# The last unit of q and k in 4 tiles of 112 tokens, the last pair of v in 8 tiles of 120, and an output with filler tokens

## The chip, the cores and the metric

The kernel runs on one core of a Trainium2 chip. A core has a matrix engine (TensorE, PE in the profile), a vector engine (VectorE, DVE), a scalar engine (ScalarE, ACT), a general engine (GpSimd, POOL) and a sync engine (SyncE, SP), which here does nothing but issue DMA transfers. Operands lie in an on-chip memory of 128 partitions, matmul results in eight PSUM banks. The metric is device time in microseconds (us) for one launch, the median of several runs.

## The reference

Four batches (B = 4) of 5056 tokens (N) with 256 channels (C) go through an attention over channels, and all 20224 resulting tokens through a soft mixture of experts with 8 experts of 4 slots.

```python
def _attn_ref(q, k, v, tau):                      # q, k, v: (4, 5056, 256)
    qn = q / (np.linalg.norm(q, axis=1, keepdims=True) + 1e-06)
    kn = k / (np.linalg.norm(k, axis=1, keepdims=True) + 1e-06)
    s = kn.transpose(0, 2, 1) @ qn / tau          # 256 x 256 a batch: a sum over all tokens
    a = softmax over the last axis of s
    return v @ a
def _moe_ref(x, phi, w1, w2):                     # x: (20224, 256), phi: (256, 32)
    logits = x @ phi
    d = softmax over the tokens (axis 0) of logits
    slots = d.T @ x                               # 32 slots, 4 for each of 8 experts
    slot_out = relu(slots @ w1[e]) @ w2[e]        # for each expert e, w1[e]: 256 x 1024
    c = softmax over the slots (axis 1) of logits
    return c @ slot_out                           # (20224, 256)
```

## The kernel before, in words

**Units.** The scores of a batch are a sum over its tokens, so q and k are read in units of 512 tokens (10 to a batch, 40 in all, `u`): a tile `raw` of 128 partitions, with 4 tiles of 128 tokens, and q and k beside each other (1 MB a unit). 5056 is 9 x 512 + 448. The tenth unit (`u % 10 == 9`, units 9, 19, 29 and 39) therefore has three tiles of 128 tokens and a half tile of 64 (`HD`), and is loaded by two DMAs: `qk3` (128 partitions, 768 KB, line 128) and `qkh` (64 partitions, 128 KB, line 129). There are five `raw` buffers, and a unit is loaded when the one five before it is done.

For each unit ACT rounds the first two tiles into `hl` (`cast`, line 202), DVE subtracts to get the remainder (`low`, line 208), PE forms the scores (`score`: lines 258 and 259 for those two tiles, line 252 for the other two, which are used unrounded), ACT squares the unit (`square`, lines 224, 226, 227) and DVE adds the squares up for the norms (`add`, lines 234, 235, 237). In a tenth unit `square` and the upper half of `add` are each split into an instruction for 128 partitions and one for 64.

**Pairs.** v is read in pairs of units, 8 tiles of 128 tokens (5 pairs to a batch, `p`), each by two DMAs of 512 KB (line 141). The fifth pair (`p % 5 == 4`) has 7 tiles of 128 and one of 64: its second half takes a DMA of 384 KB (line 143) and one of 64 KB on 64 partitions (`vh`, line 145). v is also wanted transposed: some pairs load it so (lines 151 and 153), for others PE transposes tiles (`turn`, line 406) and ACT copies them out (`turned`, line 413). `logits` (line 428) multiplies the transposed v with `M` (attention times phi) into a PSUM bank `L`. The places of L that stand for no token in a fifth pair get -1e30 by a memset (line 423). Exponentials of the logits (`weights`, `exps`) then weigh v in `gather` (line 537).

**The end.** After the last batch the slots go through the experts' weights `w1` and `w2` (16 DMAs of 1 MB). The output of a pair is formed on PE (`out_mul`, line 764), copied from PSUM by ACT (line 791) and DVE (line 793), and stored. Four pairs of a batch are stored as 128 partitions x 8 KB (lines 800 and 802, the first four pairs of batch 0 in two halves). The fifth is stored as a 768 KB piece on 128 partitions (`ob6`, line 804) and a 192 KB piece on 96 partitions (`oh`, line 805).

**What sets the order.** Every step is an entry of a `plan`, and a list `ORDER` of 1059 numbers, written out by hand, says in which order the entries are issued. Each engine works through its own instructions in that order. All loads and stores are issued by SP, in order. An instruction waits by semaphores. Eight of these (DMAHW0 to DMAHW7 in the listings below) are shared by the transfers in turn, so that a transfer also waits for the one eight before it.

Of the kernel before, what the change touches and what calls it, by code (L numbers as in the profile page):

```python
# [81 lines left out]
def colnorm_attention_soft_moe(  # L82
    ctx: ExitStack,
    tc: tile.TileContext,
    qk: bass.AP,
    qk3: bass.AP,
    qkh: bass.AP,
    v8: bass.AP,
    v7: bass.AP,
    vh: bass.AP,  # L90
    vt8: bass.AP,
    vt7: bass.AP,
    few: bass.AP,
    w1: bass.AP,
    w2: bass.AP,
    oa: bass.AP,
    ob6: bass.AP,
    oh: bass.AP,
):
# [19 lines left out]
    raws, sqs = {}, {}  # L119

    def load_qk(u, parts=((0, 4),)):
        b, i = divmod(u, UB)
        raw = apool.tile([P, 4, 2, C], F32, tag="raw", name=f"raw{u}", bufs=NRAW)
        if i < UB - 1:
            for lo, hi in parts:
                sp.dma_start(raw[:, lo:hi], qk[b, i][:, lo:hi])
        else:
            sp.dma_start(raw[:, 0:3], qk3[b])
            sp.dma_start(raw[:HD, 3], qkh[b])
        raws[u] = raw  # L130

    vs, vts = {}, {}

    def load_v(p, h):
        b, i = divmod(p, PB)
        if p not in vs:
            vs[p] = slot("v" if p < 17 else "raw", f"v{p}")
        vt = vs[p]
        lo, hi = 4 * h, 4 * h + 4
        if i < PB - 1:  # L140
            sp.dma_start(vt[:, lo:hi], v8[b, i][:, lo:hi])
        else:
            sp.dma_start(vt[:, lo : min(hi, 7)], v7[b][:, lo : min(hi, 7)])
            if h:
                sp.dma_start(vt[:HD, 7], vh[b])

    def load_vt(p, m):
        b, i = divmod(p, PB)
        t = vt_tile(p, m)
        if i < PB - 1:  # L150
            sp.dma_start(t, vt8[b, i, m])
        else:
            sp.dma_start(t[:, : 8 * P - HD], vt7[b, m])
# [44 lines left out]

    def cast(u):
        ns = NS[u]  # L200
        hl = apool.tile([P, 2, 4, C], F32R, tag="hl", name=f"hl{u}", bufs=3)
        act.copy(hl[:, :ns, 0::2, :], raws[u][:, :ns])  # L202
        hls[u] = hl

    def low(u):
        ns = NS[u]
        hl = hls[u]
        dve.tensor_tensor(  # L208
            hl[:, :ns, 1::2, :], raws[u][:, :ns], hl[:, :ns, 0::2, :].bitcast(F32), op=ALU.subtract
        )  # L210

    sqtag = {}
# [7 lines left out]

    def square(u):
        sq = apool.tile([P, 4, 2, C], F32, tag=f"sq{sqtag[u]}", name=f"sq{u}")
        if u % UB < UB - 1:
            act.activation(sq, raws[u], AF.Square)  # L224
        else:
            act.activation(sq[:, 0:3], raws[u][:, 0:3], AF.Square)
            act.activation(sq[:HD, 3], raws[u][:HD, 3], AF.Square)
        sqs[u] = sq

    def add(u, lo, hi):  # L230
        b, i = divmod(u, UB)
        a, s = sqs[b * UB], sqs[u]
        if i == UB - 1 and hi == 4:
            dve.tensor_tensor(a[:, lo:3], a[:, lo:3], s[:, lo:3], op=ALU.add)
            dve.tensor_tensor(a[:HD, 3], a[:HD, 3], s[:HD, 3], op=ALU.add)
        else:
            dve.tensor_tensor(a[:, lo:hi], a[:, lo:hi], s[:, lo:hi], op=ALU.add)  # L237

    def score(u, j):
        b, i = divmod(u, UB)  # L240
        if "S" not in st[b]:
            st[b]["S"] = [bank(S0, f"S{b}_0"), bank(S1, f"S{b}_1")]
            st[b]["open"] = [True, True]
        pc = HD if i == UB - 1 and j == 3 else P
        for m in range(2):
            sm = st[b]["S"][m]
            cols = slice(P * m, P * m + P)
            first = st[b]["open"][m]
            st[b]["open"][m] = False
            if j >= NS[u]:  # L250
                raw = raws[u]
                pe.matmul(  # L252
                    sm[:, :C], raw[:pc, j, 1, cols], raw[:pc, j, 0, :], start=first, stop=False, skip_group_check=True
                )
# [146 lines left out]
    def turn(p, h, m, tb):  # L401
        tp = bank(tb, f"vTp{p}_{h}_{m}")
        n = 0
        for jj in range(4):
            pc = HD if p % PB == PB - 1 and h == 1 and jj == 3 else P
            pe.transpose(tp[:, n : n + pc], vs[p][:pc, 4 * h + jj, P * m : P * m + P], ident[:pc, :pc])  # L406
# [11 lines left out]
    def logits(p, lb):  # L418
        b, q = divmod(p, PB)
        M = st[b]["M"]  # L420
        L = bank(lb, f"L{p}")[:, : 8 * S].rearrange("p (j s) -> p j s", s=S)
        if q == PB - 1:
            dve.memset(L[HD:, 7, :], -1e30)
        for m in range(2):
            x = vts[p, m].rearrange("p (j w) -> p j w", w=P)
            for g in range(G):
                n = 7 if q == PB - 1 and g >= 2 else 8
                pe.matmul(  # L428
                    L[S * g : S * g + S, :n, :],
                    M[:, m, :],  # L430
                    x[:, :n, S * g : S * g + S],
                    start=m == 0,
                    stop=m == 1,
                )
        Ls[p] = L
# [316 lines left out]
    ots, ops = {}, {}  # L752
# [21 lines left out]
    def out_evict(b, p, hf, g):  # L774
        if (b, p) not in ots:
            ots[b, p] = slot(OT[b * PB + p], f"o{b}_{p}")
        ot = ots[b, p]
        if p < PB - 1:
            dst = ot.rearrange("p q (w c) -> p (q w) c", w=2).rearrange("p (x gh) c -> p gh x c", x=2)
            dst = dst[:, 2 * g : 2 * g + 2]  # L780
            src = ops[b, p, hf, g]
            if hf is None:
                src = src.rearrange("p h (x c) -> p h x c", x=2)
            else:
                dst = dst[:, :, hf]
        else:
            lo, step = (2 * g, 1) if g < 2 else (g + 2, 2)
            dst = ot[:, lo : lo + step + 1 : step, :]
            src = ops[b, p, hf, g]
        if g % 2 == 0:  # L790
            act.copy(dst, src)  # L791
        else:
            dve.tensor_copy(dst, src)  # L793

    def store(b, p, hf):
        ot = ots[b, p]
        if p < PB - 1:
            o2 = ot.rearrange("p (x q) c -> p x (q c)", x=2)
            if hf is None:
                sp.dma_start(oa[b, p], o2)  # L800
            else:
                sp.dma_start(oa[b, p][:, hf], o2[:, hf])
        else:
            sp.dma_start(ob6[b], ot[:, 0:6])
            sp.dma_start(oh[b], ot[:96, 6:8])
# [49 lines left out]
    for p in range(14):  # L855
# [6 lines left out]
        b, gi, x, n = group(p)  # L862
# [185 lines left out]
    t = 41.0  # L1048
# [13 lines left out]
    for x in ORDER:  # L1062
        key, _, f, a = plan[x]
# [66 lines left out]
```

## Time and profile before

| | |
|---|---|
| median of 3 runs | 304.97 us (303.45 to 307.35) |
| the profiled execution | 304.32 us, of which the span from first to last instruction is 302.5 us |
| granted TensorE clock, mean | 0.957 |
| busy share of the span | PE 86%, DVE 77%, ACT 65%, POOL 9% |
| DMA | 110.38 MB, 365 GB/s over the span (89.29 MB read, 20.71 MB written) |

The profile gives for each engine the time it was busy, in total and in 40 slices of the span; PEclk is the clock granted to TensorE in each slice, in tenths of full speed, and the DMA row the mean busy share of the core's 16 DMA engines. Groups of instructions are listed by line, engine, operation and tile, with count, total and mean duration. A wait is put down to the instruction or transfer that came last before the waiting engine went on. A matmul's ends are modelled, so a busy PE need not be at its peak.

### The profile page before, as it was taken

How to read it: one execution, taken by the hardware profiler on the slowest of the kernel's cores; microseconds unless marked ns; L12 is line 12 of the kernel's file. 1: busy time of each engine (PE TensorE's matmuls, PEld its weight loads, DVE VectorE, ACT ScalarE, POOL GpSimd, SP SyncE). 2: the span in 40 equal slices, each digit the busy share in tenths (PEclk: the TensorE clock that was granted, in tenths of full speed). 3: DMA queues.
4: the chain of work that ended last, by engine and by line, in shares of the span. 5: the costliest groups of instructions: out<-in, count | busy, mean ns of one | idle time of the engine just before them, and what ended most of it. 6: DMA issues, size and time to landing. Idle time of an engine off the chain costs nothing. (4 is left out here: it accounts for less than half of the span.)

```text
span 302.5 us, 5958 instructions
## 1 busy us (share of the span) xinstructions
PE 260.6 (86%) x2358; PEld 199.4 (66%) x2358; DVE 233.2 (77%) x387; ACT 196.1 (65%) x290; POOL 28.1 (9%) x18
## 2 busy tenths in 40 slices
PE   4999899999999988998999999999989999984000
PEld 3788687877768874875887687777655588763000
DVE  1599959999989979986999999567887547997000
ACT  2996969798879694675886976366840526865000
POOL 0000002000002403000222000133202030000000
PEclk9999799999999999999999999999999999999555
DMA  6999999999999998799899989699999718999996
GB/s 237 427 430 415 374 405 420 371 389 366 423 398 360 417 390 319 280 356 422 281 407 405 385 310 378 248 351 422 406 347 400 305 71 341 404 422 399 420 430 261
DMA packets 21707, 110.38 MB, mean 365 GB/s; under 512 B 2608, under 2 KB 2864, under 8 KB 13616
## 3 DMA queue, kind: packets, MB, share of 16 engines
q1 hardware_dynamic: 21680, 110.01, 92.4%
q8 instruction: 18, 0.29, 0.4%
q14 instruction: 9, 0.07, 0.1%
HBM read 89.29 MB, written 20.71 MB: 364 GB/s over the span
## 5 line engine op out<-in xcount | busy, mean ns | idle before, releaser
L252 PE MATMUL S<-raw 128*128 128x256 f32 (+1 forms) x328 | 82.4, 391 | 6.4 <-DMA raw<-in_qk_dram 4.8
L237 DVE TENSOR_TENSOR sq<-sq,sq 128x1024 f32<-128x1024 f32 (+1 forms) x59 | 81.2, 1393 | 3.2 <-ACT sq L224 2.3
L224 ACT ACTIVATE sq<-raw 128x2048 f32<-128x2048 f32 x36 | 68.7, 1914 | 14.9 <-DMA raw<-in_qk_dram 9.4
L252 PEld LDWEIGHTS S<-raw 128*128 128x128 f32 (+1 forms) x328 | 60.4, 195 | 17.1 <-DMA raw<-in_qk_dram 5.9
L258 PE MATMUL S<-hl 128*128 128x512 f32 x156 | 64.7, 444 | 1.8 <-DVE hl L208 1.8
L208 DVE TENSOR_TENSOR hl<-raw,hl 128x1024 fp32r<-128x1024 f32 x39 | 49.0, 1271 | 8.4 <-ACT hl L202 8.3
L202 ACT CAST hl<-raw 128x1024 fp32r<-128x1024 f32 x39 | 40.4, 1044 | 7.1 <-DMA raw<-in_qk_dram 4.8
L259 PE MATMUL S<-hl 128*128 128x256 f32 x156 | 44.0, 282 | 0.0
L258 PEld LDWEIGHTS S<-hl 128*128 128x128 f32 x156 | 29.6, 190 | 10.5 <-DVE hl L208 2.6
L259 PEld LDWEIGHTS S<-hl 128*128 128x128 f32 x156 | 29.8, 191 | 0.6
L406 PE MATMUL vTp<-ident,v 128*128 128x128 f32 (+1 forms) x160 | 23.4, 277 | 1.7 <-DMA v<-in_v_dram 1.7
L537 PE MATMUL G<-v,dn 128*32 128x256 f32 (+1 forms) x320 | 23.3, 382 | 0.0
L406 PEld LDWEIGHTS vTp<-ident,v 128*128 128x128 f32 (+1 forms) x160 | 18.2, 141 | 6.7 <-issue 3.0
L764 PE MATMUL op_None<-so,cT 32*128 32x256 f32 x256 | 19.6, 397 | 2.3 <-ACT o L791 1.2
L305 POOL TENSOR_TENSOR rn<-rn,half 128x4 f32<-128x4 f32 x4 | 6.8, 1701 | 154.5 <-DVE rn L300 119.8
L793 DVE COPY o<-op_None 128x512 f32<-128x512 f32 x32 | 20.0, 679 | 1.3 <-issue 1.0
L791 ACT COPY o<-op_None 128x512 f32<-128x512 f32 x32 | 17.1, 591 | 5.1 <-PE op_None L764 1.9
L764 PEld LDWEIGHTS op_None<-so,cT 32*128 32x128 f32 x256 | 15.1, 184 | 6.4 <-PE op_None L764 3.2
L428 PE MATMUL L<-vt,M 128*32 128x256 f32 (+1 forms) x272 | 18.2, 381 | 1.1 <-issue 1.1
L413 ACT COPY vt<-vTp 128x512 f32<-128x512 f32 (+1 forms) x28 | 15.8, 576 | 4.0 <-PE vTp L406 2.8
L537 PEld LDWEIGHTS G<-v,dn 128*32 128x32 f32 (+1 forms) x320 | 12.4, 109 | 6.4 <-issue 1.2
L635 POOL TENSOR_TENSOR nat<-nat,cm 128x1280 f32<-128x1280 f32 x4 | 11.2, 2803 | 30.8 <-DVE cm L632 17.5
(119 smaller groups left out, 284.2 us busy)
## 6 DMA issues: line engine op xcount, KB each, us to landing
raw<-in_qk_dram SPq DMA_DIRECT2D x35, 1024.0 KB, 9.1
v<-in_v_dram SPq DMA_DIRECT2D x36, 512.0 KB, 8.3
w<-in_moe_w_dram SPq DMA_DIRECT2D x16, 1024.0 KB, 9.0
out_dram<-o SPq DMA_DIRECT2D x12, 1024.0 KB, 9.5
vt<-in_vt_dram SPq DMA_DIRECT2D x16, 512.0 KB, 9.5
out_dram<-o SPq DMA_DIRECT2D x8, 512.0 KB, 4.1
raw<-in_qk_dram SPq DMA_DIRECT2D x4, 768.0 KB, 8.0
out_dram<-o SPq DMA_DIRECT2D x4, 768.0 KB, 8.0
```

The costliest lines, as they stand in the source:

```text
L202: act.copy(hl[:, :ns, 0::2, :], raws[u][:, :ns])
L208: dve.tensor_tensor(hl[:, :ns, 1::2, :], raws[u][:, :ns], hl[:, :ns, 0::2, :].bitcast(F32), op=ALU.subtract)
L224: act.activation(sq, raws[u], AF.Square)
L237: dve.tensor_tensor(a[:, lo:hi], a[:, lo:hi], s[:, lo:hi], op=ALU.add)
L252: pe.matmul(sm[:, :C], raw[:pc, j, 1, cols], raw[:pc, j, 0, :], start=first, stop=False, skip_group_check=True)
L258: pe.matmul(sm, hl[:, j, 2, cols], rhs, start=first, stop=False, skip_group_check=True)
L259: pe.matmul(sm[:, :C], hl[:, j, 3, cols], hl[:, j, 0, :], start=False, stop=False, skip_group_check=True)
L406: pe.transpose(tp[:, n : n + pc], vs[p][:pc, 4 * h + jj, P * m : P * m + P], ident[:pc, :pc])
L428: pe.matmul(L[S * g : S * g + S, :n, :], M[:, m, :], x[:, :n, S * g : S * g + S], start=m == 0, stop=m == 1,)
L537: pe.matmul(gp[S * g : S * g + S, :C], dn[:pc, x, j, :], vt[:pc, j, :], start=x == 0 and j < G, stop=x == n - 1 and j >= G,)
L764: pe.matmul(ops[b, p, hf, g][:, h, :], cT[b][S * g : S * g + S, 4 * i : 4 * i + 4, :].rearrange("s j t -> s (j t)"), so[S * g : S * g + S] ...
L793: dve.tensor_copy(dst, src)
```

## The change

The 448 tokens of a tenth unit become 4 tiles of 112 (`PQ`), the 960 tokens of a fifth pair of v 8 tiles of 120 (`PV`). The unit is one DMA of 896 KB on 112 partitions, the pair two DMAs of 480 KB on 120 partitions. The host passes the arrays `qk7` and `v7` in that shape; `qkh` and `vh` are gone. `cast`, `low`, `square`, `add` and `score` run on 112 partitions, with one instruction where there were two. `turn` transposes 120 columns at a time, `logits` reads tiles of 120 tokens, where the fourth group of each has 24 tokens in place of 32, and the memset fills the 8 empty columns of that group in all 8 tiles. `gather` runs over 120 partitions. The output of a fifth pair is copied and stored like any other, as 8 tiles of 128 tokens of which the last 8 are filler, in one DMA of 1024 KB; the host drops the filler. `ORDER` is as it was.

```diff
@@ load_qk
-            sp.dma_start(raw[:, 0:3], qk3[b])
-            sp.dma_start(raw[:HD, 3], qkh[b])
+            sp.dma_start(raw[:PQ], qk7[b])
@@ load_v
-            sp.dma_start(vt[:, lo : min(hi, 7)], v7[b][:, lo : min(hi, 7)])
-            if h:
-                sp.dma_start(vt[:HD, 7], vh[b])
+            sp.dma_start(vt[:PV, lo:hi], v7[b][:, lo:hi])
@@ cast (low likewise)
+        n = P if u % UB < UB - 1 else PQ
-        act.copy(hl[:, :ns, 0::2, :], raws[u][:, :ns])
+        act.copy(hl[:n, :ns, 0::2, :], raws[u][:n, :ns])
@@ square
-            act.activation(sq[:, 0:3], raws[u][:, 0:3], AF.Square)
-            act.activation(sq[:HD, 3], raws[u][:HD, 3], AF.Square)
+        act.activation(sq[:n], raws[u][:n], AF.Square)
@@ add
-            dve.tensor_tensor(a[:, lo:3], a[:, lo:3], s[:, lo:3], op=ALU.add)
-            dve.tensor_tensor(a[:HD, 3], a[:HD, 3], s[:HD, 3], op=ALU.add)
+        dve.tensor_tensor(a[:n, lo:hi], a[:n, lo:hi], s[:n, lo:hi], op=ALU.add)
@@ turn
-            pc = HD if p % PB == PB - 1 and h == 1 and jj == 3 else P
+            pc = PV if p % PB == PB - 1 else P
@@ logits
-            dve.memset(L[HD:, 7, :], -1e30)
+            dve.memset(L[S * (G - 1) :, :, w - P :], -1e30)
...
-                n = 7 if q == PB - 1 and g >= 2 else 8
+                n = min(S, w - S * g)
                 pe.matmul(
-                    L[S * g : S * g + S, :n, :],
+                    L[S * g : S * g + S, :, :n],
@@ gather
-            pc = HD if q == PB - 1 and j == 7 else P
+            pc = PV if q == PB - 1 else P
@@ store
-            sp.dma_start(ob6[b], ot[:, 0:6])
-            sp.dma_start(oh[b], ot[:96, 6:8])
+            sp.dma_start(oa[b, p], o2)
```

Three places show what this does to the engines' instructions. SP, where unit 9 is loaded (`raw_232`) between unit 8 (before it) and unit 10 (`raw_270`, `raw_269` after the change), before and then after; in brackets what a transfer waits for:

```order
L156 DMA few_sb<-in_few_dram 128x67
L128 DMA raw_232<-in_qk_dram 128x1536 [waits DVE_49,DMAHW6_49,PE_49,Activation_49]
L129 DMA raw_232<-in_qkh_dram 64x512 [waits DMAHW7_49]
L126 DMA raw_270<-in_qk_dram 128x2048 [waits DVE_49,DMAHW0_49,PE_49,Activation_49]
L141 DMA v_272<-in_v_dram 128x1024 [waits DMAHW1_49]
```

```order
L150 DMA few_sb<-in_few_dram 128x67
L125 DMA raw_232<-in_qk_dram 112x2048 [waits DVE_49,DMAHW6_49,PE_49,Activation_49]
L123 DMA raw_269<-in_qk_dram 128x2048 [waits DVE_49,DMAHW7_49,PE_49,Activation_49]
L137 DMA v_271<-in_v_dram 128x1024 [waits DMAHW0_49]
```

The transfer of 64 partitions is gone, nothing else changed place, and from here on every transfer waits for a semaphore one further back in the turn of eight.

SP at the end of the program, where the last pairs are stored, before and after:

```order
L800 DMA out_dram<-o_0_2754 128x2048 [waits DMAHW7_49]
L800 DMA out_dram<-o_3_2910 128x2048 [waits DMAHW0_49,DVE_49,Activation_49]
L804 DMA out_dram<-o_4_2925 128x1536 [waits DMAHW1_49,DVE_49,Activation_49]
L805 DMA out_dram<-o_4_2925 96x512 [waits DMAHW2_49]
L1116 UNCONDITIONAL_BRANCH
```

```order
L785 DMA out_dram<-o_0_2737 128x2048 [waits DMAHW4_49]
L785 DMA out_dram<-o_3_2891 128x2048 [waits DMAHW5_49,DVE_49,Activation_49]
L785 DMA out_dram<-o_4_2906 128x2048 [waits DMAHW6_49,DVE_49,Activation_49]
L1086 UNCONDITIONAL_BRANCH
```

The last two transfers are one, of full size.

DVE, where the squares of unit 19 (`sq_702`, `sq_697` after) are added and the logits `L` of a fifth pair masked, before and after:

```order
L456 TENSOR_REDUCE mxs_1_729<-L_664 128x1
L237 TENSOR_TENSOR sq_356<-sq_356,sq_702 128x1024
L234 TENSOR_TENSOR sq_356<-sq_356,sq_702 128x512
L235 TENSOR_TENSOR sq_356<-sq_356,sq_702 64x512
L423 MEMSET L_755 64x32
L208 TENSOR_TENSOR hl_733<-raw_633,hl_733 128x4x256
```

```order
L447 TENSOR_REDUCE mxs_1_723<-L_659 128x1
L227 TENSOR_TENSOR sq_353<-sq_353,sq_697 112x1024 x2
L414 MEMSET L_748 32x8x8
L204 TENSOR_TENSOR hl_727<-raw_628,hl_727 128x4x256
```

Three additions are two, and what follows them on DVE is the same.

More of the change, by code (lines that the diff above doesn't have):

```diff
@@ L17 @@
 P, S, G = 128, 32, 4
+PQ, PV = 112, 120
 UB = 10
@@ L85, in colnorm_attention_soft_moe @@
     qk: bass.AP,
-    qk3: bass.AP,
-    qkh: bass.AP,
+    qk7: bass.AP,
     v8: bass.AP,
     v7: bass.AP,
-    vh: bass.AP,
     vt8: bass.AP,
@@ L232, in add @@
         a, s = sqs[b * UB], sqs[u]
[L233 to L237, printed above, removed]
+        n = P if i < UB - 1 else PQ
+        dve.tensor_tensor(a[:n, lo:hi], a[:n, lo:hi], s[:n, lo:hi], op=ALU.add)
     def score(u, j):
@@ L243, in score @@
             st[b]["open"] = [True, True]
-        pc = HD if i == UB - 1 and j == 3 else P
+        pc = PQ if i == UB - 1 else P
         for m in range(2):
@@ L256, in score @@
                 hl = hls[u]
-                rhs = hl[:, j, 0:2, :].rearrange("p x c -> p (x c)")
-                pe.matmul(sm, hl[:, j, 2, cols], rhs, start=first, stop=False, skip_group_check=True)
+                rhs = hl[:pc, j, 0:2, :].rearrange("p x c -> p (x c)")
+                pe.matmul(sm, hl[:pc, j, 2, cols], rhs, start=first, stop=False, skip_group_check=True)
                 pe.matmul(
-                    sm[:, :C], hl[:, j, 3, cols], hl[:, j, 0, :], start=False, stop=False, skip_group_check=True
+                    sm[:, :C], hl[:pc, j, 3, cols], hl[:pc, j, 0, :], start=False, stop=False, skip_group_check=True
                 )
@@ L796, in store @@
         ot = ots[b, p]
[L797 to L802, printed above, removed]
[L803 to L805 removed]
+        o2 = ot.rearrange("p (x q) c -> p x (q c)", x=2)
+        if hf is None:
+            sp.dma_start(oa[b, p], o2)
+        else:
+            sp.dma_start(oa[b, p][:, hf], o2[:, hf])
     def fill(b, k):
@@ L1083 @@
     x = np.stack([q, k], axis=2)
-    n9, n3 = 9 * UT, 3 * P
+    n9 = 9 * UT
     add("qk", x[:, :n9].reshape(B, 9, 4, P, 2, C).transpose(0, 1, 3, 2, 4, 5))
-    add("qk3", x[:, n9 : n9 + n3].reshape(B, 3, P, 2, C).transpose(0, 2, 1, 3, 4))
-    add("qkh", x[:, n9 + n3 :])
-    n4, n7 = 4 * 2 * UT, 7 * P
+    add("qk7", x[:, n9:].reshape(B, 4, PQ, 2, C).transpose(0, 2, 1, 3, 4))
+    n4 = 4 * 2 * UT
     add("v8", v[:, :n4].reshape(B, 4, 8, P, C).transpose(0, 1, 3, 2, 4))
-    add("v7", v[:, n4 : n4 + n7].reshape(B, 7, P, C).transpose(0, 2, 1, 3))
-    add("vh", v[:, n4 + n7 :])
+    add("v7", v[:, n4:].reshape(B, 8, PV, C).transpose(0, 2, 1, 3))
     add("vt8", v[:, :n4].reshape(B, 4, 2 * UT, 2, P).transpose(0, 1, 3, 4, 2))
@@ L1103 @@
         add(name, inputs[name])
-    flat = nc.dram_tensor("out_0_dram", (B * N * C,), F32, kind="ExternalOutput").ap()
-    cuts = np.cumsum([0, B * 4 * P * 8 * C, B * P * 6 * C, B * 96 * 2 * C])
-    shapes = [(B, 4, P, 2, 4 * C), (B, P, 6, C), (B, 96, 2, C)]
-    pats = [
[3 rows of a table removed]
-    ]
-    for x_, (lo, hi) in enumerate(zip(cuts[:-1], cuts[1:])):
-        sh = shapes[x_]
-        names = pats[x_].split("->")[1].split()
-        args.append(flat[int(lo) : int(hi)].rearrange(pats[x_], **dict(zip(names[1:], sh[1:]))))
+    out_ap = nc.dram_tensor("out_0_dram", (B, PB, P, 2, 4 * C), F32, kind="ExternalOutput").ap()
+    args.append(out_ap)
     with tile.TileContext(nc, schedule_with_timeline_sim=True) as tc:
@@ L1118 @@
     r = run_bass_kernel_spmd(nc, [arrays], core_ids=[0])
-    o = np.asarray(r.results[0]["out_0_dram"]).reshape(-1)
-    oa, ob, oh = (o[int(lo) : int(hi)].reshape(sh) for lo, hi, sh in zip(cuts[:-1], cuts[1:], shapes))
-    out = np.empty((B, N, C), np.float32)
-    out[:, :n4] = oa.reshape(B, 4, 4, S, 2, G, 2, P).transpose(0, 1, 6, 2, 5, 3, 4, 7).reshape(B, n4, C)
-    last = np.zeros((B, P, 8, C), np.float32)
-    last[:, :, [0, 1, 2, 3, 4, 6]] = ob
-    last[:, :96, [5, 7]] = oh
-    last = last.reshape(B, 4, S, G, 2, C).transpose(0, 4, 1, 3, 2, 5)
-    out[:, n4:] = last.reshape(B, 2 * UT, C)[:, : N - n4]
+    o = np.asarray(r.results[0]["out_0_dram"]).reshape(B, PB, 4, S, 2, G, 2, P)
+    o = o.transpose(0, 1, 6, 2, 5, 3, 4, 7).reshape(B, PB, 8, P, C)
+    out = np.concatenate([o[:, : PB - 1].reshape(B, n4, C), o[:, PB - 1, :, :PV].reshape(B, N - n4, C)], axis=1)
     return out.reshape(B * N, C)
```

37 lines of the change are left out of this document (15 added, 22 removed), and 3 rows, old and new, of the table pats.

## The prediction

> **What bounds the kernel now.** I first read the page's busy times and slices, to see which stage has which limit.
>
> ```profile
> PE 260.6 (86%) x2358; PEld 199.4 (66%) x2358; DVE 233.2 (77%) x387; ACT 196.1 (65%) x290; POOL 28.1 (9%) x18
> PE   4999899999999988998999999999989999984000
> DMA  6999999999999998799899989699999718999996
> ```
>
> Three stages stand out. For some 235 us PE and the DMA engines are both nearly full. In slice 33 (242 to 250 us) the DMA engines are busy for a tenth. After it the outputs are stored, PE falls to nothing, and the DMA engines are full up to the last slice. The busy times of three stretches say this in figures (columns: length; PE, PEld, DVE, ACT, POOL busy, with counts; granted clock; DMA share; GB/s):
>
> ```profile
> 60.00:110.00 50.00, 49.61 (x363) 39.05 (x362) 46.24 (x69) 42.54 (x53) 5.19 (x2) 1.00 1.01 393
> 110.00:130.00 20.00, 17.55 (x148) 12.01 (x146) 19.38 (x25) 12.32 (x17) 2.34 (x1) 1.00 0.85 324
> 255.00:300.00 45.00, 19.51 (x264) 14.99 (x257) 22.36 (x40) 17.80 (x35) 0.00 (x0) 0.78 1.00 412
> ```
>
> From 60 to 110 us PE works 49.61 of 50 us, with the DMA engines full beside it. From 110 to 130 us DVE is the fullest (19.38 of 20) and transfers have 15% to spare. From 255 us to the end only transfers count: whatever bytes are added there are paid at 412 GB/s. The end follows the last store, as SP's own wait at the very end shows, and the first store waits for the experts:
>
> ```profile
> SPq L802 <- DVE o L793: 25.7, 7, 19.5
> SPq L1116 <- DMA out_dram<-o: 13.5, 1, 13.5
> ```
>
> So a cost in the loads counts if PE feels it, and a cost in the stores counts in full. The list of waits names where PE waits for what the change touches (total us, times, longest):
>
> ```profile
> PE S L252 <- DMA raw<-in_qkh_dram: 1.5, 1, 1.5
> PE vTp L406 <- DMA v<-in_v_dram: 1.7, 3, 0.8
> ```
>
> The first is the 64-token tile of unit 9, in PE's timeline, and the clock granted in the next microseconds (columns of the second fence: length, clock, DMA share, GB/s):
>
> ```profile
> 33.48 1.20 PE L252 MATMUL S<-raw 64*128 64x256 f32 x4 [1.46 <-DMA raw<-in_qkh_dram]
> ```
>
> ```profile
> 34.00:35.00 1.00, 0.70 1.03 418
> 35.00:36.00 1.00, 0.50 1.02 410
> 36.00:37.00 1.00, 0.50 1.01 406
> 37.00:38.00 1.00, 0.59 1.11 455
> ```
>
> The stop costs 1.46 us, and the clock below 1.00 behind it a further 0.30 + 0.50 + 0.50 + 0.41 = 1.71 us of PE's work.
>
> **The change part by part.** *Instructions.* ACT's split squares become one, DVE's split additions too:
>
> ```profile
> L224 ACT ACTIVATE sq<-raw 128x2048 f32<-128x2048 f32 x36 | 68.7, 1914 | 14.9 <-DMA raw<-in_qk_dram 9.4 <-DVE sq L237 5.5
> L226 ACT ACTIVATE sq<-raw 128x1536 f32<-128x1536 f32 x4 | 5.9, 1484 | 1.2 <-DMA raw<-in_qk_dram 1.2
> L227 ACT ACTIVATE sq<-raw 64x512 f32<-64x512 f32 x4 | 2.5, 618 | 0.0
> L237 DVE TENSOR_TENSOR sq<-sq,sq 128x1024 f32<-128x1024 f32 x51 | 62.9, 1252 | 2.5 <-ACT sq L224 1.7 <-ACT sq L226 0.5
> L235 DVE TENSOR_TENSOR sq<-sq,sq 64x512 f32<-64x512 f32 x4 | 2.7, 676 | 0.0
> L234 DVE TENSOR_TENSOR sq<-sq,sq 128x512 f32<-128x512 f32 x3 | 2.0, 669 | 0.0
> ```
>
> A square took 1484 + 618 = 2102 ns and takes about 1914, if 112 partitions cost what 128 do: 4 x 0.19 = 0.75 us less. ACT is 65% busy, and PE does not wait for the squares: 0. An addition took 669 + 676 = 1345 ns and takes 1252: 0.09 us less in three units. Only unit 29's lies where DVE leads (110 to 130 us): -0.1 us; if DVE has room there, 0.
>
> PE keeps its matmuls one for one, less wide in places:
>
> ```profile
> L406 PE MATMUL vTp<-ident,v 64*128 64x64 f32 x4 | 1.1, 273 | 0.0
> L406 PE MATMUL vTp<-ident,v 128*128 128x128 f32 x156 | 22.7, 277 | 1.7 <-DMA v<-in_v_dram 1.7
> L423 DVE MEMSET L<- 64x32 f32 x4 | 0.3, 85 | 0.0
> ```
>
> 64 columns cost 273 ns, 128 cost 277, so 120 cost the same: 0. In `logits` 256 + 256 + 224 + 224 columns become 3 x 256 + 192, 960 both times: 0. The memset stays an instruction of under 0.1 us, with the same `logits` waiting behind it: 0. The filler rows of `cT` were computed before as well. Output copies have the form of the first four pairs'.
>
> *Stores.* Per batch 768 + 192 KB become 1024 KB: 4 x 64 KB = 262 KB more, at 412 GB/s +0.64 us, all of it on the path. Against that stand the 96-partition pieces, behind which the rate dips:
>
> ```profile
> 260.00:261.00 1.00, 1.00 1.00 350
> 276.00:277.00 1.00, 1.00 0.95 336
> 279.00:280.00 1.00, 1.00 1.06 367
> ```
>
> Against 412 GB/s these three microseconds lack 62 + 76 + 45 = 183 KB, 0.44 us. The likely cause are the 96-partition pieces, issued from 257.88 and from 271.54 us (SP's rows below) and carried some microseconds later. Bounds: +0.64 if the dips stay, +0.2 if they go. I take +0.2.
>
> *Loads.* The bytes are the same. What changes is the share that comes on fewer than 128 partitions: 4 x 128 + 4 x 64 = 768 KB now, 4 x 896 + 8 x 480 = 7424 KB after. No transfer of 112 or 120 partitions is in this trace, so its price needs bounds. The nearest rows are the stretches in which the 64-partition transfers are carried, the `qkh` ones in the first four rows, a `vh` alone in the last two:
>
> ```profile
> 30.00:32.00 2.00, 1.00 1.04 283
> 70.00:74.00 4.00, 1.00 1.04 334
> 124.00:126.00 2.00, 1.00 1.00 304
> 180.00:183.00 3.00, 1.00 0.97 287
> 171.00:174.00 3.00, 1.00 1.06 393
> 189.00:191.00 2.00, 1.00 0.98 395
> ```
>
> The DMA engines were busy all the time, and still moved less than 412 GB/s. The time lost is length x (412 - rate) / 412: 0.63, 0.76, 0.52, 0.91, 0.14 and 0.08, together 3.0 us.
>
> - Lower bound: partial partitions at the ends of a unit were the cause, 112 and 120 behave like 128, and 3.0 us of transfer time goes.
> - Upper bound: all 7424 KB move at the 283 GB/s of the first row. 896 KB take 3.24 us and not 2.23 (4 x 1.01), 480 KB take 1.74 and not 1.19 (8 x 0.54): +8.4 us, less the 3.0 = +5.4 us.
> - What I take lies between: the loss comes with each switch from full to part transfers, 3.0 / 8 = 0.38 us a transfer. Twelve in place of eight: +1.5 us, of which PE sees only those up to 110 us, where transfers have nothing to spare. That is four (units 9 and 19, two of pair 4) where three were: +0.4 us.
>
> [...] The 283 GB/s of the first row agrees with a slow 64; no row shows 112 or 120.
>
> *SP.* Twelve issues fewer:
>
> ```profile
> 257.50 0.33 SPq L804 DMA_DIRECT2D out_dram<-o  x1
> 257.88 1.88 SPq L805 DMA_DIRECT2D out_dram<-o  x1
> 259.87 0.39 SPq L800 DMA_DIRECT2D out_dram<-o  x1
> ...
> 271.54 1.31 SPq L805 DMA_DIRECT2D out_dram<-o  x1
> ...
> 176.67 0.47 SPq L129 DMA_DIRECT2D raw<-in_qkh_dram  x1
> ```
>
> A 64-partition transfer took 0.47 us to issue, a 96-partition one 1.88 between neighbours of 0.33 and 0.39, the next 1.31. Saved are about 8 x 0.47 us in the loads, worth nothing, as SP waits for buffers between its issues. What could cost is that 112 and 120 issue as slowly as 96 (a rival). Nothing gains a new wait; but tiles 0 to 2 of unit 9 now land with its last tile. Queued behind is `cast` on ACT, then `low` and the scores. PE stands waiting for the half tile anyway, so 0.
>
> Sum on the profiled execution: 304.32 + 0.2 + 0.4 - 0.1 = 304.8 us. That execution lies 0.65 us below the median of the three runs; on the median, 304.97 + 0.5 = 305.5 us.
>
> **The rivals.** *The part transfers are slow for their bytes* (slower): the upper bound, with all 5.4 us felt by PE, and 0.2 in the stores, gives 304.97 + 5.6 = 310.6 us. If one more stop like unit 9's comes of it (1.46 + 1.71), 313.8 us. The place is units 9 and 19 and pair 4, before transfers have room at 110 us. It passes 2% (311.1 us) only when PE stops again and its clock falls. For it speaks how low 283 GB/s is beside full engines; against it that `vh` (393 and 395 GB/s), also of 64 partitions, hardly shows.
>
> *Unit 9 no longer stops PE* (a little faster): if the loss at 30 to 32 us goes, the 0.63 us saved cut the stop, and perhaps the fall of the clock. With all of both gone (1.46 + 1.71 = 3.2), and the 0.76 us of the other early stretch (70 to 74 us), 304.97 + 0.2 - 4.0 = 301.2 us. Against it: the stop is 1.46 us, over twice the 0.63.
>
> *Slow issue*: 12 issues of 1.88 in place of 0.33 are 19 us of SP's time. Hidden where SP waits for buffers, visible in bursts, about 1.5 us in each of two batches: 308 us. Against: SP's issues also lengthen when the queue is full, so 1.88 may not be the partitions' doing.
>
> **How the numbers follow.** Forecast, no change that can be told (303.5 to 307.4): 0.60. Unit 9's stop gone (300.5 to 303.5): 0.15. Slow part transfers (307.5 to 314): 0.15, of which 0.09 past 311.1. Slow issue (306.5 to 309): 0.07. Something not seen, faster than 298.9 us: 0.03. About 2%, 6.1 us, is what a measurement here can tell from no change; the three runs span 1.3%. Faster 0.03, same 0.88, slower 0.09. Leaving out about 0.1 at each end gives 302 to 309.5 us.
>
> **What would show it.** Right: the stores last about 0.2 us longer, without the three dips; `raw` of 112 and `v` of 120 partitions move without dips of their own; stretches around them at 330 GB/s or better. Wrong: PE waiting for `raw` or `v` for over 3 us more in total, a second fall of the clock, stretches under 300 GB/s of more than 2 us, or SP issues of 1.2 us and more on lines of 112 and 120 partitions.

## Result: 6.3% slower, and all of it lies in the loads

The changed kernel takes 324.21 us (median of 4 runs, 321.38 to 328.52), the kernel before on the same chip 304.35 us: a ratio of 1.063, interval 1.057 to 1.069. Forecast was 305.5 us and no change. The profiled execution of the changed kernel is its longest run, 328.52 us; where times are compared below, medians are, and its trace serves for places and durations.

The page of the changed kernel, with its busy times and its count of packets:

```profile
PE 269.7 (83%) x2358; PEld 204.9 (63%) x2358; DVE 233.5 (71%) x383; ACT 196.7 (60%) x286; POOL 28.1 (9%) x18
...
DMA packets 20483, 110.64 MB, mean 339 GB/s; under 512 B 2408, under 2 KB 2408, under 8 KB 11432
```

PE runs the same 2358 matmuls but is busy 9.1 us longer (269.7 against 260.6), at a mean granted clock of 0.921 where it was 0.957, and DVE and ACT are busy as long as before. So nothing was added to any engine's work. Next, when the first store is issued on SP, of the kernel before and of the changed one:

```profile
247.29 2.01 SPq L802 DMA_DIRECT2D out_dram<-o  x2
```

```profile
271.46 0.35 SPq L787 DMA_DIRECT2D out_dram<-o  x1
```

The first store comes 24.2 us later, and the span is 24.2 us longer (326.7 against 302.5; by the medians the loss is 19.9 us). From the first store on, both kernels take 55.2 us. The loss is there before a byte of output moves. The three stretches that the prediction showed of before, now of the changed kernel, the last one moved along with the stores (length; PE, PEld, DVE, ACT, POOL busy; granted clock; DMA share; GB/s):

```profile
60.00:110.00 50.00, 46.71 (x327) 35.23 (x326) 40.30 (x61) 36.33 (x44) 4.07 (x2) 0.90 0.94 324
110.00:130.00 20.00, 17.70 (x141) 13.34 (x140) 19.27 (x23) 13.75 (x21) 3.47 (x2) 1.00 0.99 394
279.00:324.00 45.00, 19.65 (x269) 15.15 (x262) 22.50 (x41) 17.96 (x35) 0.00 (x0) 0.76 1.00 418
```

The stores run at 418 GB/s (412 before). From 60 to 110 us the DMA engines are busy 94% of the time and move 324 GB/s, where they moved 393 before. Around the 112- and 120-partition transfers the rate is lower still, with the DMA share at 1.0:

```profile
30.00:35.00 5.00, 2.03 (x9) 1.36 (x8) 4.61 (x4) 2.86 (x2) 0.00 (x0) 1.00 0.98 278
75.00:80.00 5.00, 3.32 (x24) 2.42 (x16) 4.79 (x7) 2.98 (x5) 0.00 (x0) 1.00 1.02 226
195.00:200.00 5.00, 3.82 (x20) 3.08 (x18) 1.19 (x2) 2.85 (x2) 0.00 (x0) 1.00 1.01 226
```

PE meets part of this as waits for data. The list of waits (total us, times, longest), first a line of before, then three of the changed kernel:

```profile
PE S L252 <- DMA raw<-in_qk_dram: 4.8, 3, 4.2
```

```profile
PE S L242 <- DMA raw<-in_qk_dram: 7.3, 3, 4.1
PE vTp L396 <- ACT vt L403: 5.4, 1, 5.4
PE vTp L396 <- DMA v<-in_v_dram: 5.2, 4, 2.8
```

The waits for `raw` and `v` were 4.8 + 1.5 + 1.7 = 8.0 us (the last two in the prediction) and are 7.3 + 5.2 = 12.5 us, 4.5 us more. That is a small part of the 24.2 us; the list puts other waits down to ACT (here one of 5.4 us). PE's timeline at unit 9, and at the second half of the first pair of v on 120 partitions:

```profile
35.30 1.15 PE L242 MATMUL S<-raw 112*128 112x256 f32 x4 [2.43 <-DMA raw<-in_qk_dram]
81.15 1.06 PE L396 MATMUL vTp<-ident,v 120*128 120x120 f32 x4 [2.83 <-DMA v<-in_v_dram]
```

Unit 9 stops PE for 2.43 us, where it was 1.46 us, and the half pair of v stops it for 2.83 us. The clock falls behind both stops, after the first to 0.50 from 37 to 39 us (from 35 to 37 us before), after the second in a longer stretch:

```profile
82.00:86.00 4.00, 3.66 (x20) 1.80 (x22) 1.48 (x3) 2.37 (x2) 0.00 (x0) 0.50 1.02 424
86.00:90.00 4.00, 4.00 (x19) 2.95 (x12) 2.87 (x5) 1.03 (x2) 0.00 (x0) 0.50 1.02 423
```

Summed over the packets in the trace, the 16 DMA engines were busy 17.9 us longer up to the first store (248.2 us against 230.3, the mean of the engines). In the other 6.3 of the 24.2 us they moved nothing. Part of that idle time lies behind this fall of the clock: from 92 to 94 us the DMA share is 0.62, from 94 to 96 us it is 0.05.

Two readings offer themselves: the transfers themselves became so slow that they explain all of it, or they became somewhat slow and PE's stops, with the clock at half, multiplied that. The experiments had to tell these apart.

### The profile page after: what moved, and what is told of

The parts are those of the page before. It is cut to its first block, busy times and chain, and to the rows that moved or that the text cites. A ratio compares the mean times of both kernels' runs of the same rounds, so it can differ in the third digit from the quotient of the medians.

```text
span 326.7 us, 5935 instructions
## 1 busy us (share of the span) xinstructions
PE 269.7 (83%) x2358; PEld 204.9 (63%) x2358; DVE 233.5 (71%) x383; ACT 196.7 (60%) x286; POOL 28.1 (9%) x18
## 5 line engine op out<-in xcount | busy, mean ns | idle before, releaser
L227 DVE TENSOR_TENSOR sq<-sq,sq 128x1024 f32<-128x1024 f32 (+3 forms) x63 | 87.0, 1399 | 6.3 <-ACT sq L220 5.9
L220 ACT ACTIVATE sq<-raw 128x2048 f32<-128x2048 f32 (+1 forms) x40 | 76.3, 1914 | 25.0 <-DMA raw<-in_qk_dram 20.1
L242 PE MATMUL S<-raw 128*128 128x256 f32 (+1 forms) x328 | 84.2, 398 | 7.4 <-DMA raw<-in_qk_dram 7.3
L248 PE MATMUL S<-hl 128*128 128x512 f32 (+1 forms) x156 | 66.9, 456 | 1.4 <-DVE hl L204 1.4
L204 DVE TENSOR_TENSOR hl<-raw,hl 128x1024 fp32r<-128x1024 f32 (+1 forms) x39 | 49.0, 1271 | 13.7 <-ACT hl L197 13.5
L197 ACT CAST hl<-raw 128x1024 fp32r<-128x1024 f32 (+1 forms) x39 | 40.4, 1045 | 11.3 <-DMA raw<-in_qk_dram 9.3
L249 PE MATMUL S<-hl 128*128 128x256 f32 (+1 forms) x156 | 44.9, 288 | 0.0
L248 PEld LDWEIGHTS S<-hl 128*128 128x128 f32 (+1 forms) x156 | 30.6, 196 | 10.1 <-DVE hl L204 2.9
L249 PEld LDWEIGHTS S<-hl 128*128 128x128 f32 (+1 forms) x156 | 31.0, 198 | 0.7
L419 PE MATMUL L<-vt,M 128*32 128x256 f32 x272 | 19.0, 396 | 5.7 <-issue 4.1
L419 PEld LDWEIGHTS L<-vt,M 128*32 128x32 f32 x272 | 8.2, 112 | 13.2 <-issue 6.2
L528 PEld LDWEIGHTS G<-v,dn 128*32 128x32 f32 (+1 forms) x320 | 12.2, 114 | 5.6 <-issue 0.8
## 6 DMA issues: line engine op xcount, KB each, us to landing
raw<-in_qk_dram SPq DMA_DIRECT2D x4, 896.0 KB, 12.1
```

Source lines behind the costliest of these rows:

```text
L197: act.copy(hl[:n, :ns, 0::2, :], raws[u][:n, :ns])
L204: dve.tensor_tensor(hl[:n, :ns, 1::2, :], raws[u][:n, :ns], hl[:n, :ns, 0::2, :].bitcast(F32), op=ALU.subtract)
L220: act.activation(sq[:n], raws[u][:n], AF.Square)
L227: dve.tensor_tensor(a[:n, lo:hi], a[:n, lo:hi], s[:n, lo:hi], op=ALU.add)
L242: pe.matmul(sm[:, :C], raw[:pc, j, 1, cols], raw[:pc, j, 0, :], start=first, stop=False, skip_group_check=True)
L248: pe.matmul(sm, hl[:pc, j, 2, cols], rhs, start=first, stop=False, skip_group_check=True)
```

## Experiments

The kernel before was timed beside each of them, on the same chip.

**The same instructions, padded loads.** The instructions stay on 112 and 120 partitions, the arrays are padded with rows of zeros in memory, and the loads run on 128 partitions: 768 KB more to read.

```diff
-            sp.dma_start(raw[:PQ], qk7[b])
+            sp.dma_start(raw, qk7[b])
...
-            sp.dma_start(vt[:PV, lo:hi], v7[b][:, lo:hi])
+            sp.dma_start(vt[:, lo:hi], v7[b][:, lo:hi])
```

> The changed kernel, but the last unit of q and k and the last pair of v are padded with zero rows in memory and loaded on all 128 partitions (4 x 128 KB and 8 x 32 KB more bytes); every instruction still works on 112 and 120 partitions. Theory A (the transfers of 112 and 120 partitions are slow): the loss of about 20 us goes, 303 to 308 us. Theory B (the loss is in the instructions on 112 and 120 partitions, in one transfer holding up the whole unit, or in the shifted turn of the semaphores): it stays, 320 to 326 us.

Measured: 304.85 us, ratio 0.992 (0.985 to 0.998) to before. The whole loss is gone, though more bytes move. Unit 9 in its trace:

```profile
32.70 1.13 PE L242 MATMUL S<-raw 112*128 112x256 f32 x4 [0.71 <-DMA raw<-in_qk_dram]
```

So neither the instructions on 112 and 120 partitions, nor the stores with filler, nor the order cost anything that can be told: the loads do. Whether the padded kernel beats the kernel before was measured once more:

> The padded kernel once more, in five rounds: whether it is faster than the kernel before. From the first run a ratio of 0.985 to 0.998. If the gain is real, 0.985 to 0.997 again; if it was chance, an interval that holds 1.000.

Measured: 305.40 us against 305.14, ratio 1.002 (0.997 to 1.007). The gain of the first measurement does not hold up: the padded kernel is as fast as the kernel before, and not faster by anything these runs can tell.

**One half of the change alone.** Only the part on q and k (`load_qk`, `cast`, `low`, `square`, `add`, `score`), then only the part on v and the output (`load_v`, `turn`, `logits`, `gather`, `store`):

```diff
 only q and k
-            sp.dma_start(raw[:, 0:3], qk3[b])
-            sp.dma_start(raw[:HD, 3], qkh[b])
+            sp.dma_start(raw[:PQ], qk7[b])
 ...
 only v and the output
-            sp.dma_start(vt[:, lo : min(hi, 7)], v7[b][:, lo : min(hi, 7)])
-            if h:
-                sp.dma_start(vt[:HD, 7], vh[b])
+            sp.dma_start(vt[:PV, lo:hi], v7[b][:, lo:hi])
 ...
```

> Only the q and k part of the change: last unit on 112 partitions, v and the output as before. By bytes on part partitions (4 x 896 KB of 7424 KB) theory A gives half of the loss, about +10 us, 314 us. If 112 partitions are harmless (they split evenly over 16) and only the 120 are slow: 304 to 306 us. Theory B gives +5 to +15 us and the same rates of transfer as before.

> Only the v and output part of the change: last pair on 120 partitions and the stores with filler, q and k as before. Theory A by bytes (8 x 480 KB): about +10 us, 314 us; if 120 partitions alone are the cause: 322 to 325 us. The output's part by itself: +0.2 to +0.6 us.

Measured: 309.90 us, ratio 1.019 (1.012 to 1.027), and 316.16 us, ratio 1.040 (1.032 to 1.048). Together 1.9% + 4.0% = 5.9%, close to the 6.3% of the whole: four transfers of 112 rows cost about a third of it, eight of 120 rows the rest. By bytes both halves would have come to about 314 us, so the bytes on part partitions do not set the price: a transfer of 112 rows costs less for its bytes than two of 120 rows.

**Rates, with nothing computed.** A kernel that leaves out the whole computation and issues 16 loads of one form after each other, form after form, then alternating ones, then stores. The load and one of the nine groups:

```diff
+    def load(i, src, k):
...
+        sp.dma_start(bufs[i][:n, :w], src)
...
+    def seg_112():
+        for i in range(NB):
+            load(i, x112[i], i)
+        drain(64)
...
```

> No computation of the reference at all, its output is arbitrary: nine groups of 16 loads each, drained in between, of 1 MB on 128 partitions, then with rows of the same length on 112, 120, 120 in rows of 4 KB, 96 and 64 partitions, then 128 alternating with 112, with 120 (4 KB rows) and with 64; at the end 20 stores of 1 MB. Theory A: 128 alone about 415 GB/s, 112 and 120 alone 280 to 330, 64 alone about 280. A variant, A2, that only the mixing of forms is slow: 112, 120 and 64 alone above 390 GB/s, the mixed groups under 350. Theory B: all above 390 GB/s.

Stretches of its trace (length; clock; DMA share; GB/s), in turn loads of 128, 112, 120 (8 KB a row), 120 (4 KB), 96 and 64 rows, then stores of 128:

```profile
5.00:40.00 35.00, 1.00 1.01 423
50.00:90.00 40.00, 1.00 1.01 298
105.00:165.00 60.00, 1.00 0.95 214
180.00:205.00 25.00, 1.00 0.97 226
220.00:260.00 40.00, 1.00 1.01 245
275.00:305.00 30.00, 1.00 1.02 206
...
460.00:495.00 35.00, 1.00 1.01 427
```

The form is slow by itself, with no compute engine at work beside it. 120 rows move at half the rate of 128 and hardly faster than 64. By these rates 917.5 KB on 112 rows take 3.08 us where they would take 2.17 at 423 GB/s (+0.91), and 491.5 KB on 120 rows 2.17 where they would take 1.16 (+1.01).

The three groups that alternate with transfers of 128 rows (8 KB a row) ran at 360 GB/s with 112 rows, 322 with 120 (4 KB) and 267 with 64 (8 KB). At 423 GB/s for the 128 rows, that is 0.8, 1.1 and 2.2 us for each part transfer, where the same sum for 64 rows alone gives 1.3 us. The first two cost about what they cost alone, the third clearly more: a first sign that the neighbours count.

**Which rows are slow.** Again loads only, 8 KB a row, with other counts of rows; 120 rows with a pitch of 8 and of 9 KB in memory; stores of 120, 112 and 126 rows.

```diff
-    for rows in (128, 112, 120, 96, 64):
+    for rows in (126, 117, 108, 80, 32, 16, 120):
...
+    xp = np.zeros((16, 120, 9 * C), np.float32)
+    xp[:, :, : 8 * C] = arrays["in_x120_dram"]
...
```

> Loads of nothing but one form, 16 after each other per stretch, 8 KB a row, no computation at all (the output holds none of the reference's values); then stores of 120, 112 and 126 rows. The run before gave 423 GB/s for 128 rows, 298 for 112, 214 for 120, 245 for 96, 206 for 64. [...]

In turn 126, 117, 108, 80, 32 and 16 rows, 120 with a pitch of 8 KB, 120 with 9 KB, then stores of 120, 112 and 126:

```profile
10.00:50.00 40.00, 1.00 0.88 334
60.00:100.00 40.00, 1.00 0.82 347
107.00:147.00 40.00, 1.00 0.76 308
158.00:195.00 37.00, 1.00 1.02 235
205.00:220.00 15.00, 1.00 1.02 206
228.00:240.00 12.00, 1.00 1.03 109
255.00:305.00 50.00, 1.00 0.95 219
330.00:375.00 45.00, 1.00 0.95 205
400.00:425.00 25.00, 1.00 0.95 390
432.00:466.00 34.00, 1.00 1.00 336
476.00:530.00 54.00, 1.00 0.88 299
```

First the DMA share. With 126, 117, 108 and 120 rows it is 0.88, 0.82, 0.76 and 0.95, near 14, 13, 12 and 15 sixteenths (0.875, 0.81, 0.75, 0.94); with 80, 32 and 16 rows it is 1.02 and 1.03. From these shares I estimate that the first four kept 14, 13, 12 and 15 of the 16 engines at work. Then the rates. 108 rows at a share of 0.76 (308) beat 120 rows at 0.95 (219). Neither the count of rows nor the share can bring this about, and the pitch in memory does not either (205 with 9 KB).

The counts tried rest on a guess of mine, called collisions from here on: that the engines of a transfer get in each other's way, by how the rows are shared out among them. No trace shows which rows an engine carries, nor a collision. 126, 117 and 108 rows, which are 14, 13 and 12 times 9, come near what so many engines would carry at their share of 423 GB/s, an estimated 370, 344 and 317 (334, 347 and 308 measured, within some 10%); 120 rows, 15 times 8, come to 219 where that estimate is 397. But the guess names no cause for the 298 of 112 rows or the 245 of 96, and the stores are ordered otherwise: 120 rows store at 390 GB/s, 112 at 336, and 126, the fastest of the three as a load, at 299. So the counts of rows that are slow are shown; why they are is not.

**Transfer time without a slow form.** The padded kernel with twelve more loads of 128 rows into buffers that nobody reads, of 9.8 us in all: what the part transfers take longer than the padded ones by the rates above. Then the same with these twelve on 112 and 120 rows. The code of the second kernel; in the first, the spare loads run on all 128 rows:

```diff
+    def spare(w, n):
+        t = keep.tile([P, 728], F32, tag="spare", name=f"spare{len(extra)}", bufs=2)
+        extra.append(t)
+        sp.dma_start(t[:n, :w], qk[0, 0].rearrange("p a b c -> p (a b c)")[:n, :w])
...
             sp.dma_start(raw, qk7[b])
+            spare(576, PQ)
...
             sp.dma_start(vt[:, lo:hi], v7[b][:, lo:hi])
+            spare(728, PV)
```

> The padded kernel of the first experiments (all loads on 128 partitions) with twelve more loads on 128 partitions into spare buffers that nobody reads: 295 KB behind each batch's last load of q and k, 373 KB behind each half load of the batch's last pair of v. At 423 GB/s that is 4 x 0.70 + 8 x 0.88 = 9.8 us of transfer time, what the 112- and 120-row transfers take more than the padded ones by the measured rates (4 x (3.08 - 2.48) + 8 x (2.17 - 1.24) = 9.8 us), without any slow form. Theory (the loss is transfer time, and PE's stops with their falls of the clock about double it): 318 to 326 us, against 304.9 of the padded kernel and 324.2 of the changed one, with the granted clock at 0.5 in two stretches or more before the stores. Rival (transfer time costs what it is, and something else in 112 and 120 partitions costs the rest): 311 to 315 us. Rival (transfer time is mostly hidden): under 309 us.

> The padded kernel with the same twelve loads into spare buffers as in the run before, but these spare loads now on 112 rows (4) and 120 rows (8) instead of 128; everything the computation needs still comes on 128 partitions. They move a little less (258 and 349 KB instead of 295 and 373). The spare loads on 128 rows gave 314.3 us. If the form matters only by its own rate (298 and 226 GB/s), they take 0.17 and 0.67 us longer each, 6.0 us in all: 320 us. If part transfers also slow the full ones behind them, by half again to twice as much, 323 to 327 us. If the rows do not matter inside the kernel, and the changed kernel lost the rest because PE waited for those very transfers, 313 to 315 us.

Measured: 314.29 us, ratio 1.032 (1.025 to 1.040) with 128 rows; 326.42 us, ratio 1.071 (1.063 to 1.079) with 112 and 120. Two things follow. 9.8 us of plain transfer time cost 314.29 - 305.40 = 8.9 us over the padded kernel, about one for one: the theory that PE's stops and clock falls double a loss is wrong here, although the granted clock fell as well (0.933 in the profiled execution, 0.962 in that of the padded kernel). And fewer bytes on 112 and 120 rows cost 12.1 us more than on 128, where the rates of transfers of one kind explain 6.0: inside the kernel a part transfer costs about twice that price (1.4 to 2.6 times, by the intervals of the two ratios).

**A part transfer among full ones.** Loads only: stretches in which every fifth transfer is a part one, the others being 128 rows of 8 KB.

```diff
+        for i in range(30):
+            load(i, x128[i % 16] if i % 5 < 4 else part(i // 5))
```

> Loads only, nothing is computed. Five stretches of 30 loads, in each of which every fifth is a part transfer among full ones (128 rows of 8 KB, 2.48 us each at 423 GB/s): the part is 128 rows of 4 KB (the control), 112 rows of 8 KB, 120 rows of 4 KB that lie end to end in memory, 120 rows of 4 KB out of rows of 8 KB (as the changed kernel reads v), 64 rows of 2 KB. Then 16 of the fourth kind alone. The load stage of the changed kernel held 18.6 us more DMA time than that of the padded one, 1.55 us a part transfer, where the rates of transfers of one kind in a row explain 0.6 and 0.93. Theory one (a part transfer among full ones leaves the engines out of step, and its collisions go on in the full transfers behind it): a part costs 1.5 to 3 us among full ones, so 340 to 375 GB/s with 112 rows and 340 to 370 with both kinds of 120, while 64 rows, of which every engine carries the same number with the same delay, cost about 0.3 us and leave 412 or more. Theory two (the price of the part alone, 0.91 and 1.01 us): 393 GB/s with 112, 388 with both kinds of 120. Theory three (reading 4 KB out of 8 KB in memory is what is slow): 388 where the rows lie end to end, 365 or less where not, and alone well under 226. The control gives 420 by all three.

In turn the control (128 rows of 4 KB), 112 rows, 120 end to end, 120 out of rows of 8 KB, 64 rows of 2 KB; the last row is 120 out of rows of 8 KB alone:

```profile
20.00:65.00 45.00, 1.00 1.02 422
90.00:140.00 50.00, 1.00 1.01 397
160.00:215.00 55.00, 1.00 1.02 369
250.00:300.00 50.00, 1.00 1.01 387
325.00:365.00 40.00, 1.00 1.01 398
385.00:410.00 25.00, 1.00 0.94 238
```

A group of 5.11 MB takes 12.9 us at 397 and 12.1 at 422: 112 rows cost 0.8 us here. By the same sum 120 end to end cost 1.6, 120 out of 8 KB 1.0, 64 rows 0.6. A mixed answer: 112 rows and 120 out of 8 KB cost the price of the part alone, 120 end to end came dearer, and so did 64 rows, at twice the 0.3 expected by the theory that makes the others dear. None gives the 2 us of the kernel.

**The kernel's loads without the kernel.** All loads of the changed kernel, and of the padded one, in their order and into their buffers, with nothing computed, then 20 stores of zeros.

```diff
-        f(*a)
+        if f in (load_qk, load_v, load_vt, load_few, load_w1, load_w2):
+            f(*a)
...
```

> The changed kernel with every load in its order and into its buffers, and nothing else: no engine computes, so a load waits only until the one before it in its buffer has landed; then 20 stores of a buffer of zeros. To be compared with the same of the padded kernel. Up to the first store's issue, the padded loads alone should take about 90.4 MB / 420 GB/s = 215 us. If the part transfers cost here what they cost in rows of one kind, the changed kernel's loads take 9.8 us longer than the padded ones; then the 18.6 us of DMA time that it held more come of how the computation paces the loads. If their neighbours in the list (4 KB and 3.8 KB rows, small transfers ahead) bring it about, 15 to 20 us longer with nothing computed.

> The same of the padded kernel: all its loads in their order and into their buffers, nothing computed, 20 stores of zeros. About 215 us up to the first store; the difference to the run before is the price of the part transfers in this list, 9.8 us by their own rates, 15 to 20 us if their neighbours make it dearer.

The first store's issue in the first, and in the second:

```profile
224.52 0.35 SPq L1051 DMA_DIRECT2D out_dram<-zero  x1
```

```profile
202.90 0.35 SPq L1051 DMA_DIRECT2D out_dram<-zero  x1
```

21.6 us apart, without a single matmul. Between the two full kernels lie 324.21 - 305.40 = 18.8 us. So the list of loads by itself has a loss of that size, and the full kernel shows about 3 us less of it. Since the padded list also moves 786 KB more (1.9 us at 417 GB/s), a part transfer costs (21.6 + 1.9) / 12 = 2.0 us in this list. The stretch from 70 to 75 us in each:

```profile
70.00:75.00 5.00, 0.00 (x0) 0.00 (x0) 0.00 (x0) 1.00 1.00 244
```

```profile
70.00:75.00 5.00, 0.00 (x0) 0.00 (x0) 0.00 (x0) 1.00 1.04 418
```

**What makes it dear.** Loads only, with neighbours like those in the kernel. A `full` is 128 rows of 8 KB, a `half` rows of 4 KB, 128 of them where no count is given; `part` is a `half` (the control), 120 rows of 4 KB or 112 rows of 8 KB.

```diff
+    def seg_few112():
+        for i in range(6):
+            for _ in range(4):
+                full()
+            sp.dma_start(few[i], x128[i][:, :67])
+            nxt(x112[i])
...
+    def seg_short(part):
+        for i in range(6):
+            full()
+            half()
+            half()
+            full()
+            part(i)
...
+    def seg_pair():
+        for i in range(6):
+            half(120)
+            half(120)
+            for _ in range(4):
+                full()
```

> Loads only, nothing computed. What makes a part transfer cost about 1.8 us in the kernel's list of loads (21.6 us over twelve, without any computation), where the same transfer behind four full ones cost 0.9 (112 rows) and 1.1 us (120 rows of 4 KB out of 8 KB)? Five stretches of six groups: four full transfers (128 rows of 8 KB), a small one of 268 bytes a row, then 112 rows of 8 KB; two full and three 4 KB transfers of 128 rows (control); the same with 120 rows in the last of the three; two full, two of 4 KB and 112 rows of 8 KB; a pair of 120 rows of 4 KB, then four full. Theory (what lies ahead puts the engines out of step, and the collisions then last longer): the dear price, about 2 us, in the stretches with the small transfer (360 GB/s) or with 4 KB neighbours (343 with 120 rows, 347 with 112). Rival (the neighbours' form does not matter): the price of before, 393, 378 and 386 GB/s. For the pair 363 if each costs 1.0, 319 if each costs 2. The control gives 415 to 420.

In turn 112 rows behind a small transfer, the control, 120 rows and 112 rows as `part`, and the pair:

```profile
30.00:90.00 60.00, 1.00 1.02 343
110.00:150.00 40.00, 1.00 1.02 416
166.00:214.00 48.00, 1.00 1.02 349
240.00:305.00 65.00, 1.00 1.01 265
325.00:395.00 70.00, 1.00 1.00 288
```

With the group's bytes, against 422 or 416 GB/s: 112 rows behind a small transfer cost 15.0 - 12.2 = 2.8 us, 120 rows in a group with short rows 10.4 - 8.7 = 1.7, 112 rows in such a group 15.3 - 9.8 = 5.5, the pair 18.0 - 12.3 = 5.7, or 2.9 each. The dear price is there, and in three of the four stretches dearer than expected. So a part transfer has no price of its own: 112 rows cost 0.8 to 5.5 us, 120 rows 1.0 to 2.9, by what is queued around them.

The trace also keeps the time of every packet, here of every row, and shows who pays. In the stretch of the pair, rows of 8 KB come only in full transfers; they take 432 ns on average, where those of the control take 313. Over the 512 rows of a group and 16 engines that is 3.8 of the 5.7 us. In the lists of loads, too, full transfers are slowed: rows of 3840 bytes come only in transfers of v transposed on 128 partitions, and take 211 ns beside the part transfers and 152 in the padded list. So a part transfer costs its own slow rows and slows the full transfers near it. That the engines are out of step is the reading under which these were tried; that the neighbours decide and share the cost is shown, their mechanism is not.

## Why the prediction was wrong

- **Instructions** (0, at most -0.1 us): right. The rows of the changed kernel, grouped by form:

```profile
L220 ACT ACTIVATE sq<-raw 112x2048 f32<-112x2048 f32 x4 | 7.6, 1911 | 3.2 <-DMA raw<-in_qk_dram 3.2
L396 PE MATMUL vTp<-ident,v 120*128 120x120 f32 x32 | 5.3, 303 | 4.6 <-DMA v<-in_v_dram 4.6
```

  A square on 112 partitions takes 1911 ns (1914 assumed). The transposes' mean is 303 ns where 277 was taken, 0.8 us over 32 of them: 21 of them take 264 to 268 ns, and the four at 81 us, where the granted clock is 0.50, 407 to 463. And the padded kernel, with the same instructions, is as fast as the kernel before.
- **Stores** (+0.2 us): nothing speaks against it. The stage takes 55.2 us in both traces, so neither bound (+0.2, +0.64) can be told from nothing by one profile of each.
- **Loads** (loss of 0.38 us with each switch, twelve for eight, +1.5 us, of which PE sees +0.4): this is the step that failed, in three places. *The price*: I took 0.38 us for a switch between forms, whatever follows. In fact the rows of a part transfer themselves move slowly, and so do those of the full transfers near it. With transfers of one kind after each other 112 partitions lose 0.91 and 120 lose 1.01 us; in this list it is 2.0 us, five times the 0.38. *The upper bound* (283 GB/s for all part bytes): it held for 112 rows with nothing but their kind around them (298) and failed for 120 (205 to 238), which no row of before was like; and even bounds by the transfer's own rate miss what it does to its neighbours. *What PE feels*: only the transfers up to 110 us were to count, a quarter of the loss. But of the 21.6 us between the two lists of loads 18.8 show in the full kernels. When twelve transfers take 23.5 us more, the 15% to spare from 110 to 130 us are 3 us, and the changed kernel's row for that stretch has the DMA share at 0.99: the room is used up, and the later ones count as well.
- **120 rows on an estimated 15 engines**, for which the sum has no term. The loads alone have 120 rows at a DMA share of 0.95, where 128 have 1.01, and the count of packets agrees, of before:

```profile
DMA packets 21707, 110.38 MB, mean 365 GB/s; under 512 B 2608, under 2 KB 2864, under 8 KB 13616
```

  Of those under 512 bytes 128 are the rows of `few`. The other 2480 are 16 for each of its 155 transfers. After the change 2280 are left for 143 transfers, 8 short of 16 each, and eight of these have 120 rows. With 15 engines in place of 16, 491.5 KB would take an estimated 0.08 us more than the 1.16 at 423 GB/s, 0.6 us over eight: the small part of the price, as such a transfer lost 1.01 us among its own kind.
- **SP** (0) and the rival *slow issue* (0.07): refuted. 112 and 120 rows issue in about the time of 128 (0.33 to 0.43 us for the loads around these):

```profile
67.53 0.33 SPq L125 DMA_DIRECT2D raw<-in_qk_dram  x1
67.92 0.43 SPq L139 DMA_DIRECT2D v<-in_v_dram  x1
```

  The argument against the rival, that issues also lengthen without it, has its rows in the kernel before: 128-partition stores of line 800 took from 0.33 to 1.57 us to issue. That a full queue does it is not shown.

- The rival *unit 9 no longer stops PE* (0.15) goes the other way: 2.43 us instead of 1.46. With padded loads the stop is 0.71 us, and even that was worth no time that can be told.
- The rival *slow part transfers* (0.15; 310.6 or 313.8 us) named the cause and the sign. Its size was off by the price: 8.4 us over full rate (5.4 after taking off the 3.0 of before) for what is 23.5 us in the list. And its condition was wrong: it wanted a second stop of PE and a fall of the clock to pass 2%. Both came, yet the loads alone, with no PE to stop, already cost more than the kernel lost by its median. The argument against it, that the 64-row `vh` stretches ran at 393 and 395 GB/s, came from transfers of 64 KB that cost an estimated fraction of a microsecond each (0.6 us was measured for one of 128 KB among full ones).

My first theory behind the result, that PE's stops double the loss, fell with the spare loads of 128 rows (314.29 us where 318 to 326 were expected). What the clock adds in a single execution stays open: in the profiled one, which is 4.3 us longer than the median, the DMA engines stood idle 6.3 us more than before, in part behind the fall of the clock.

## What to carry to other kernels

Where the DMA engines are full for most of a kernel, cost a transfer's form before its bytes: here 112 and 120 partitions, with nothing else around them, moved at 0.7 and about half the rate of 128 (298 and 205 to 238 against 423 GB/s), slowed the full transfers beside them (432 ns for a row in place of 313), and rows of zeros up to 128 were worth more than the bytes they added (305.40 us against 324.21). If the trace of before has no transfer of the new form, its nearest rows are no bound; a list of loads alone, in the kernel's order and with nothing computed, shows the loss directly (21.6 us here). And a fall of the clock next to a loss need not be its cause.

## What the runs showed of the hardware that was not expected

- 120 partitions load at 205 to 238 GB/s, about half of 128 (423) and less than 108 (308), 117 (347) or 126 (334). Of the other counts tried 96, 80, 64, 32 and 16 were slow too (245, 235, 206, 206 and 109); 112 lies between at 298. Why is not shown.
- The same part transfer of 112 rows costs from 0.8 to 5.5 us depending on what is queued around it. Part transfers also slow the full ones near them: beside pairs of 120-row transfers a row of a full one took 432 ns for 313.
- Stores of 120 rows do not suffer as their loads do: 390 GB/s, where the loads of the same form run at 219.
- The granted clock stood at 0.50 for 8 us behind a stop of PE of 2.83 us (82 to 90 us in the changed kernel), and the time lost by the median, 18.8 us over the padded kernel, was still no more than the 21.6 us of the loads alone.
